# One column block of x by a transposing DMA in the opening of a gated state-space and feed-forward kernel

## The chip, the cores and the metric

The kernel runs on one core of a Trainium2 chip. The metric is the device time of one execution in microseconds; the figure shown is the median of three timed runs. A profiled execution of the same kernel was recorded as well, and its trace is what is read below. Engines are named as the profile names them: PE is TensorE (PEld its weight loads), DVE is VectorE, ACT is ScalarE, POOL is GpSimd, SP is SyncE, which only issues DMAs here. A "q" behind an engine's name means its instruction queue, as in ACTq.

## The reference

```python
x = A_x                                    # 1 x 2048 x 448, bf16
g = sigmoid((x * gate_w).sum(-1, keepdims=True))
# a: a diagonal complex state space of 448 states
dt = exp(log_dt); Lam_bar = exp(dt * Lam)
B_bar = ((Lam_bar - 1.0) / Lam)[:, None] * Bmat
h[t] = Lam_bar * h[t-1] + x[t] @ B_bar.T           # for all 2048 steps
a = 2.0 * real(h @ Cmat.T) + x * Dskip
# b: a feed-forward block, 448 -> 1792 -> 448
b = silu(x @ w1) @ w2
out = g * a + (1 - g) * b
```

Every product with x on TensorE needs x with its 448 features on the partitions, so x is transposed once. The feed-forward block's first product (x times `w1`, then Silu) is the first large piece of work.

## The kernel before

**Layout.** Two neighbouring time steps stand in one row: x is seen as 1024 rows of 896 numbers (`x2`), the even step in columns 0 to 447, the odd one in 448 to 895. `XT` holds x transposed: for each of even and odd three blocks of 128 features and a remainder block, for 1024 rows each. A feature dimension of 448 is three blocks of 128 and 64 left over. The remainder block holds columns 384 to 511 of x2 for the even steps, so that its lower 64 partitions are even features 384 to 447. `XR` is a copy of the 64 remainder features on the other 64 partitions: products with the remainder run as two 64-row matmuls beside each other, one from `XT` (lower half) and one from `XR` (upper half).

**The order of the work** is written out by hand. A tracker records every operation with the buffers it reads and writes (`T.op`, `T.dma`) and puts a wait in front of it where needed; each engine then runs its own list in the order of recording. Plain loads are recorded by `ld` (line 226), transposing DMAs by `ldt` (line 229, always on SP's queue). Two queues issue DMAs, SP's and ACT's.

**The opening**, on which the change bears, handles the first 512 rows of the even steps ("half 0"):

- Lines 275 to 294 issue the first loads, alternately on SP and ACT. `XH` is the first half of the buffer `XN`, seen as four blocks k of 128 rows. XA0 to XA3 are pieces of these four blocks. XB0 (line 282, ACT) holds columns 256 to 511 of blocks 0 and 1, XB1 (line 286, SP) columns 384 to 511 of blocks 2 and 3. Between them go the loads of `w1` (`W1E`): columns 0 to 767 first (`W1Ej0` in two pieces, `W1Ej1`, `W1Ej2`), then on SP and ACT in turn the remainder rows (`W1Er0` on SP, `W1Er1` on ACT), columns 768 to 1279 (`W1Ed0` on SP, `W1Ed2` on ACT), the remainder rows of the later columns (`W1Es0`, `W1Es1`), and columns 1280 to 1791 (`W1Ee0`, `W1Ee1`).
- Line 292 is a one-column Exp that makes ACT load its table of Exp early. Lines 300 and 301 issue, on ACT, the loads of `gate_w` and `Dskip`, each broadcast to 128 partitions (`GWB`, `DB`).
- Line 308 makes SP wait for both remainder loads (`gE`). Then come SP's transposing DMAs: half 1 of the even steps (`XTe1`, `XTer1`), four for the B matrices (`BT`), the plain load of the rest of half 0 (`load_xn(0)`, columns 512 to 895), four for the odd steps, and the plain load of half 1.
- Half 0 of the even steps is transposed on TensorE instead: `turn_k` (line 491) transposes one 128x128 block of `XH` into PSUM, and VectorE copies it to `XT` (lines 501 and 507). The blocks' keys are XTe00, XTe01, XTe02 and, for the remainder block, XTe03.
- `ffn1_first` (line 433) multiplies feature blocks 0, 1 and 2 with the first six column blocks of `w1` as they arrive, between the transposes. Line 472 is a small product that puts the state space's vectors on the partitions; from it VectorE and ACT make the coefficients (`dt`, `phf`, `ar`, `mag`, then `phr`, `fr` and on to the phases, which GpSimd also works on).
- Lines 535 and 536 transpose the remainder block, `turned_x(3)` (line 570) copies it to `XT`, and line 571 copies its lower half from PSUM to the upper half of `XR`. Line 572 is a one-column Silu that loads ACT's Silu table.
- `ffn1_rem` (line 447) adds the remainder's products, three pairs, and `ffn1_act` (line 455) applies Silu to two PSUM banks at a time.

From then on `pair` and `lanes` (line 365) run all further products of `w1` and of B as pairs of 64-row matmuls; the first such pair reads `W1Ed0`, `W1Ed2`, and for its remainder `W1Es0` and `W1Es1`. Later the gate reads `XH` (`gate`, line 650), and `skip` (line 658) multiplies it with `DB`; `xblock` says which loads these wait for.

Of the kernel before, what the change touches and what calls it, by code (L numbers as in the profile page):

```python
# [8 lines left out]
AF = mybir.ActivationFunctionType  # L9
# [141 lines left out]
def gated_mix(nc, A_x, A_Lambda_re, A_Lambda_im, A_B_re, A_B_im, A_C_re, A_C_im, A_log_dt,  # L151
              A_Dskip, B_x, B_w1, B_w2, gate_w, out):
    with ExitStack() as ctx:
        E = ctx.enter_context
        T = Tracker(nc, ctx)

        def sb(name, shape, dtype):
            return E(nc.sbuf_tensor(name, list(shape), dtype))

        x2 = A_x[0].rearrange("(k i) d -> k (i d)", i=2)  # L160
        out2 = out[0].rearrange("(k i) d -> k (i d)", i=2)

        XT = sb("XT", [128, 8, NK], BF16)
# [7 lines left out]
        XR = sb("XR", [128, NK], BF16)  # L171
# [4 lines left out]
        XN = sb("XN", [128, 2 * NKT * D], BF16)  # L176
        AT = [sb(f"AT{i}", [128, NFB, 512], BF16) for i in range(2)]
        OT = sb("OT", [128, 4, D], BF16)
        GWB = sb("GWB", [128, D], BF16)
        DB = sb("DB", [128, D], BF16)  # L180
        JK = sb("JK", [128, 2], BF16)
# [7 lines left out]
        ID = sb("ID", [128, 128], BF16)  # L189
# [5 lines left out]
        HP = sb("HP", [128, 1], F32)  # L195
# [25 lines left out]
        ps = E(nc.psum_tensor("ps", [128, 8, 512], F32))  # L221
# [3 lines left out]
        def ld(eng, dst, src, key, group=None):  # L225
            return T.dma(eng, lambda e: e.dma_start(dst, src), writes=[key], group=group)  # L226

        def ldt(dst, src, key, reads=(), group=None, also=()):
            return T.dma("sp", lambda e: e.dma_start_transpose(dst, src), reads=reads,
                         writes=[key, *also], group=group)  # L230
# [4 lines left out]
        def swap_xr(eng, h, odd):  # L235
            hs = slice(h * 512, (h + 1) * 512)
            if odd:
                T.op(eng, lambda e: e.tensor_copy(XR[0:64, hs], XT[64:128, 7, hs]), reads=XO[h][1],
                     writes=[f"XR{h}b"])
            else:  # L240
                T.op(eng, lambda e: e.tensor_copy(XR[64:128, hs], XT[0:64, 3, hs]), reads=XE[h][1],
                     writes=[f"XR{h}a"])
# [7 lines left out]
        def row(v):  # L250
            return v.rearrange("(o n) -> o n", o=1)

        XH = XN[:, 0:8 * D].rearrange("p (k c) -> p k c", k=4)
        XA = ["XA0", "XA1", "XA2", "XA3", "XB0", "XB1"]
        FA, FB = 768, 1280
        x0 = x2[0:512, 0:512].rearrange("(k p) c -> p k c", p=128)

        def ld_w(eng, j, f0=0, f1=FA, key=""):
            ld(eng, W1E[:, j, f0:f1], B_w1[j * 128:(j + 1) * 128, f0:f1], f"W1Ej{j}{key}")
# [4 lines left out]
        def ld_w3(eng, j0, j1, f0, f1, key):  # L264
            ld(eng, W1E[:, j0:j1, f0:f1], B_w1[j0 * 128:j1 * 128, f0:f1].rearrange("(j p) f -> p j f", p=128),
               f"W1E{key}{j0}")

        def ld_wr(eng, c, later):
            p = slice(64 * c, 64 * c + 64)
            if later:  # L270
                return ld(eng, W1E[p, 3, 384:896].rearrange("p (n f) -> p n f", n=2),
                          B_w1[384:448, FA:].rearrange("p (n c f) -> p n c f", n=2, c=2)[:, :, c, :], f"W1Es{c}")
            return ld(eng, W1E[p, 3, 0:384], B_w1[384:448, 384 * c:384 * c + 384], f"W1Er{c}")

        for k, eng in enumerate(("sp", "act")):
            ld(eng, XH[:, k, 0:256], x0[:, k, 0:256], XA[k])
        for c, eng in enumerate(("sp", "act")):
            ld_w(eng, 0, 384 * c, 384 * c + 384, c)
        for k, eng in ((2, "sp"), (3, "act")):
            ld(eng, XH[:, k, 0:384], x0[:, k, 0:384], XA[k])  # L280
        ld_w("sp", 1)
        ld("act", XH[:, 0:2, 256:512], x0[:, 0:2, 256:512], XA[4])
        for i, (eng, v) in enumerate((("sp", A_log_dt), ("sp", A_Lambda_re), ("act", A_Lambda_im))):
            ld_row(eng, i, v)
        ld_w("act", 2)
        ld("sp", XH[:, 2:4, 384:512], x0[:, 2:4, 384:512], XA[5])
        gE = [ld_wr(eng, c, False) for c, eng in enumerate(("sp", "act"))]
        ld_w3("sp", 0, 2, FA, FB, "d")
        ld_w3("act", 2, 3, FA, FB, "d")
        for c, eng in enumerate(("sp", "act")):  # L290
            ld_wr(eng, c, True)
        T.op("act", lambda e: e.activation(JK[:, 0:1], HP[:, :], AF.Exp), reads=["HP"], writes=["JK0"])
        ld_w3("sp", 0, 1, FB, F_FF, "e")
        ld_w3("act", 1, 3, FB, F_FF, "e")
        BTK = [f"BT{i}" for i in range(4)] + ["BTz"]
# [1 line left out]
        def ld_b(dst, src, key):  # L297
            ld("act", dst[:, :], row(src).partition_broadcast(128).rearrange("p o n -> p (o n)"), key)

        ld_b(GWB, gate_w, "GW")  # L300
        ld_b(DB, A_Dskip, "DB")

        def load_xn(h):
            c0 = 0 if h else 512
            ld("sp", XN[:, 8 * h * D:8 * (h + 1) * D].rearrange("p (k c) -> p k c", k=4)[:, :, c0:],
               x2[h * 512:(h + 1) * 512, c0:].rearrange("(k p) c -> p k c", p=128), f"XN{h}")

# [5 lines left out]
        for i, src in enumerate((A_B_re, A_B_im)):  # L313
# [15 lines left out]
             writes=["IOTA"])  # L329
# [128 lines left out]
        def ffn1(c, f0=0, ahead=None):  # L458
            for fb in range(f0, NFB, 2):
                pair(*ffn1_pair(c, fb), last=(c == 3 and fb == NFB - 2))  # L460
                if ahead and fb == 8:
                    ahead()
                yield
# [23 lines left out]
        xp = [ps[:, b, 0:256].bitcast(BF16) for b in PB]  # L487

        def turn_k(j, k, b=None):
            b = PB[j] if b is None else b  # L490
            T.op("pe", lambda pe: pe.transpose(  # L491
                ps[:, b, 0:256].bitcast(BF16)[:, k * 128:(k + 1) * 128], XH[:, k, j * 128:(j + 1) * 128], ID[:, :]),
                reads=[XA[k if j < 2 or (j == 2 and k > 1) else 4 + k // 2], "ID"], writes=[f"ps{b}"])

        def turn_x(j, i):
            for k in (2 * i, 2 * i + 1):
                turn_k(j, k)
# [6 lines left out]
        def turned_x(j, i=None, b=None):  # L504
            c, key = (slice(0, 512), f"XTe0{j}") if i is None else (slice(256 * i, 256 * i + 256), f"XTe0{j}{i}")
            b = PB[j] if b is None else b
            T.op("dve", lambda e: e.tensor_copy(XT[:, j, c], ps[:, b, 0:256].bitcast(BF16)[:, c]),
                 reads=[f"ps{b}"], writes=[key])
# [13 lines left out]
        for k in (2, 3):  # L522
# [7 lines left out]
            reads=["pv", "ps7"], writes=["PV"])  # L530
# [1 line left out]
            turn_x(2, i)  # L532
        turned_x(2)
        next(first)
        for i in range(2):
            turn_x(3, i)

        names = {}

        def pc(n):  # L540
            if n not in names:
                names[n] = len(names)
            return names[n]

        def col(n):
            i = pc(n)
            return P[:, i, :]
# [7 lines left out]
        def pts(o, a, s1, s2, op0, op1, ra):  # L555
            T.op("dve", lambda e: e.tensor_scalar(col(o), a, s1, s2, op0, op1), reads=ra, writes=[o])

        def ptt(o, a, b, op, ra):
            T.op("dve", lambda e: e.tensor_tensor(col(o), a, b, op), reads=ra, writes=[o])

        def pact(o, a, f, ra, scale=1.0, bias=0.0):
            T.op("act", lambda e: e.activation(col(o), a, f, bias=bias, scale=scale),
                 reads=ra, writes=[o])
# [3 lines left out]
            col("phf"), LIM, 1.0 / TWO_PI, col("dt"), ALU.mult, ALU.mult), reads=["PV", "dt"], writes=["phf"])  # L567
        ptt("ar", col("dt"), LRE, ALU.mult, ["dt", "PV"])
        pact("mag", col("ar"), AF.Exp, ["ar"])
        turned_x(3)  # L570
        T.op("dve", lambda e: e.tensor_copy(XR[64:128, 0:512], xp[3][0:64, :]), reads=["ps7"], writes=["XR0a"])
        T.op("act", lambda e: e.activation(JK[:, 0:1], HP[:, :], AF.Silu), reads=["HP"], writes=["JK0"])
        pts("phr", col("phf"), MAGIC, -MAGIC, ALU.add, ALU.add, ["phf"])
        ptt("fr", col("phf"), col("phr"), ALU.subtract, ["phf", "phr"])
        pts("nfr", col("fr"), -1.0, None, ALU.mult, ALU.bypass, ["fr"])
# [6 lines left out]
            reads=["f2"] + SGN, writes=["f2s"])  # L582
# [55 lines left out]
        def xblock(b):  # L638
            v = XN[:, 4 * b * D:4 * (b + 1) * D].rearrange("p (k c) -> p k c", k=4) if b > 1 else \
                XH[:, :, b * D:(b + 1) * D]  # L640
            return v, [*(XA if b < 2 else []), *([f"XN{b // 2}"] if b else [])]

        def block(tile):
            return tile // 4 if tile > 7 else tile % 2
# [1 line left out]
        def gate():  # L646
            for b in range(4):
                v, ks = xblock(b)
                o, ws = xg(b)
                T.op("dve", lambda e, v=v, o=o: e.tensor_tensor(  # L650
                    o, v, GWB[:, :].unsqueeze(1).to_broadcast([128, 4, D]), ALU.mult),
                    reads=ks + ["GW"], writes=ws)
                yield

        def skip():
            for b in range(4):
                v, ks = xblock(b)
                T.op("dve", lambda e, v=v: e.tensor_tensor(
                    v, v, DB[:, :].unsqueeze(1).to_broadcast([128, 4, D]), ALU.mult),
                    reads=ks + ["DB"], writes=[f"XD{b}"] + ks)  # L660
                yield
# [12 lines left out]
             writes=["BTz"] + BTK[2:4])  # L674
# [486 lines left out]
        f = ffn1(2)  # L1161
# [100 lines left out]
```

## Time and profile before

| what | value |
|---|---|
| timed runs | 136.61, 136.64, 136.76 us; median 136.64 |
| profiled execution | 136.72 us, of which the span from first to last instruction is 135.3 |
| TensorE | busy 131.9 us, 97% of the span |
| VectorE | busy 114.2 us, 84% |
| ScalarE | busy 93.7 us, 69% |
| GpSimd | busy 15.1 us, 11% |
| DMA | 24928 packets, 11.95 MB; 16851 packets under 512 B |

Times in the trace count from the first instruction of the span. The span is shorter than the execution's time by what lies before and after it. The 40 slices of the page are 3.4 us each, and a digit is the busy share in tenths:

```profile
PE   7899999999999999999999999999999999999993
DMA  4999979999897220000122000000000000222123
```

TensorE is busy in every slice from the second on; the DMA engines are busy in the first dozen slices and hardly afterwards. Matmuls are pipelined, so that a busy TensorE is not TensorE at its peak. The granted TensorE clock was 1.0 over the whole span.

### The profile page before, as it was taken

The numbers are of one execution on the slowest core, as the hardware profiler recorded it, in microseconds if no ns is written. First come the engines' busy times: TensorE is split into PE (matmuls) and PEld (weight loads), VectorE is DVE, ScalarE is ACT, GpSimd is POOL, SyncE is SP. The second block draws the span as 40 slices with busy tenths as digits, with TensorE's granted clock in tenths as the row PEclk, the third lists the DMA queues.
The fourth block names the chain that finished last, engine by engine and source line by source line (L and its number), as shares of the span: only waits on it lengthen the run. The fifth ranks groups of instructions, "written<-read, shape, count | busy, mean of one in ns | idle before, by whom it ended". The sixth has DMA issues, their size and how long they took to land.

```text
span 135.3 us, 2630 instructions
## 1 busy us (share of the span) xinstructions
PE 131.9 (97%) x1072; PEld 65.7 (49%) x1073; DVE 114.2 (84%) x152; ACT 93.7 (69%) x146; POOL 15.1 (11%) x32
## 2 busy tenths in 40 slices
PE   7899999999999999999999999999999999999993
PEld 7554444444444554444445544445555555555552
DVE  1467898917899798999999999999999999994554
ACT  0369888899939999768999597797113437879200
POOL 7108768050000000000000000000000000000000
DMA  4999979999897220000122000000000000222123
GB/s 109 273 278 162 157 153 244 181 286 300 251 184 123 55 62 0 0 0 0 44 56 60 5 0 0 0 5 0 0 0 0 0 0 7 100 89 81 68 78 126
DMA packets 24928, 11.95 MB, mean 88 GB/s; under 512 B 16851, under 2 KB 24406, under 8 KB 24918
## 3 DMA queue, kind: packets, MB, share of 16 engines
q1 hardware_dynamic: 22996, 10.43, 32.3%
q10 hardware_dynamic: 1922, 1.37, 3.6%
q8 instruction: 8, 0.13, 0.4%
q14 instruction: 2, 0.02, 0.0%
HBM read 5.51 MB, written 1.84 MB: 54 GB/s over the span
## 4 chain that ended last, share of the span: by engine, by line
PE 94%; DMA 3%; DVE 1%; ACTq 1%; issue 0%
PE ps L365 44%; PE ps L794 16%; PE ps L809 16%; PE ps L1047 15%; DMA XN<-in_A_x_dram 3%; PE ps L433 3%; DVE TMPS L1071 1%; ACTq L226 1%; PE ps L491 1%; PE ps L447 1%; PE ps L472 0%
## 5 line engine op out<-in xcount | busy, mean ns | idle before, releaser
L365 PE MATMUL ps<-XT,W1E 64*128 64x512 bf16 x325 | 41.3, 376 | 0.0
L455 ACT ACTIVATE AT<-ps 128x1024 bf16<-128x1024 f32 x28 | 28.2, 1019 | 7.4 <-PE ps L365 7.2
L365 PEld LDWEIGHTS ps<-XT,W1E 64*128 64x128 bf16 x325 | 16.9, 94 | 19.0 <-ACT AT L455 0.3
L365 PE MATMUL ps<-XT,BT 64*128 64x512 bf16 x156 | 22.4, 376 | 0.0
L809 PE MATMUL ps<-W,AT 64*128 64x448 bf16 x224 | 21.5, 349 | 0.0
L794 PE MATMUL ps<-W,AT 128*128 128x448 bf16 x112 | 21.4, 353 | 0.0
L794 PEld LDWEIGHTS ps<-W,AT 128*128 128x128 bf16 x112 | 10.9, 98 | 10.5 <-issue 0.4
L809 PEld LDWEIGHTS ps<-W,AT 64*128 64x128 bf16 x224 | 10.9, 94 | 10.4
L838 ACT ACTIVATE BT<-ps,GT 128x448 bf16<-128x448 f32 x8 | 5.1, 634 | 13.2 <-PE ps L794 13.2
L894 DVE SCALAR_TENSOR_TENSOR HS<-VE,P,ps 128x512 bf16<-128x512 bf16 (+1 forms) x13 | 9.6, 780 | 3.9 <-PE ps L365 3.9
L365 PEld LDWEIGHTS ps<-XT,BT 64*128 64x128 bf16 x156 | 8.1, 94 | 9.3 <-DVE HS L894 0.4
L938 DVE TENSOR_TENSOR_SCAN G<-P,Q 128x1024 f32<-128x1024 f32 (+1 forms) x6 | 11.4, 1923 | 0.0
L1047 PE MATMUL ps<-CO,VE 128*128 128x448 bf16 (+2 forms) x63 | 11.1, 332 | 0.0
L1047 PE MATMUL ps<-CO,HS 128*128 128x448 bf16 x56 | 11.1, 352 | 0.0
L365 PE MATMUL ps<-XR,W1E 64*128 64x512 bf16 x25 | 9.2, 376 | 0.0
L1047 PEld LDWEIGHTS ps<-CO,VE 128*128 128x128 bf16 x63 | 6.0, 98 | 4.8
L1047 PEld LDWEIGHTS ps<-CO,HS 128*128 128x128 bf16 x56 | 5.5, 98 | 5.1
L891 DVE TENSOR_TENSOR Q<-G,COS 128x2048 bf16<-128x2048 f32 (+1 forms) x4 | 7.0, 1755 | 0.1
L891 DVE TENSOR_TENSOR Q<-G,SIN 128x2048 bf16<-128x2048 f32 (+1 forms) x4 | 7.0, 1750 | 0.0
L856 ACT ACTIVATE VE<-ps 128x1024 bf16<-128x1024 f32 x6 | 6.1, 1020 | 1.2 <-PE ps L365 1.2
L858 ACT ACTIVATE ps<-VE,P 128x1024 f32<-128x1024 bf16 x6 | 6.7, 1118 | 0.2
L894 DVE SCALAR_TENSOR_TENSOR VE<-HS,P,FP 128x512 bf16<-128x512 bf16 (+1 forms) x7 | 6.6, 976 | 0.1
(123 smaller groups left out, 179.1 us busy)
## 6 DMA issues: line engine op xcount, KB each, us to landing
W<-in_B_w_dram SPq DMA_DIRECT2D x2, 784.0 KB, 6.6
XN<-in_A_x_dram SPq DMA_DIRECT2D x1, 896.0 KB, 5.1
out_dram<-OT SPq DMA_DIRECT2D x8, 112.0 KB, 1.7
out_dram<-TMPS SPq DMA_DIRECT2D x7, 112.0 KB, 1.7
HS<-HS SPq DMA_DIRECT2D x4, 128.0 KB, 2.3
XN<-in_A_x_dram SPq DMA_DIRECT2D x1, 384.0 KB, 3.7
W1E<-in_B_w_dram SPq DMA_DIRECT2D x1, 256.0 KB, 5.5
W1E<-in_B_w_dram ACTq DMA_DIRECT2D x1, 256.0 KB, 5.0
```

The lines of the kernel that those rows point to most:

```text
L365: ins = pe.matmul(ps[:, bank, :], w(p, j), xh(odd, h, j, p), start=start and j == js[0], stop=stop and j == js[-1], skip_group_check=seeded)
L433: T.op("pe", lambda pe, fb=fb, bank=bank, j=j, h=h, c=c: pe.matmul(ps[:, bank, c], W1E[:, j, ff(fb) * 128:(ff(fb) + 1) * 128], XT[:, j, c] ...
L455: T.op("act", lambda e: e.activation(a[:, fb:fb + n, :], ps[:, bank:bank + n, :], AF.Silu), reads=[f"ps{bank + i}" for i in range(n)], wri ...
L794: ins = pe.matmul(ps[:, bank, 0:D], a[:, fb, q * 128:(q + 1) * 128], W2[:, ff(fb), :], start=(first and fb == 0), stop=(fb == NFB - 1), sk ...
L809: ins = pe.matmul(ps[:, bank, 0:D], a[p, fb, q * 128:(q + 1) * 128], W2[p, ff(fb), :], start=(start and fb == 0), stop=(not start and fb = ...
L838: T.op("act", lambda e: e.activation(bs(tile), ps[:, bank, 0:D], AF.Copy, scale=sc), reads=[f"ps{bank}", "GT2" if h else "GRI"], writes=ks)
L856: T.op("act", lambda e: e.activation(VE[:, m:m + 2, hs], ps[:, b[0]:b[0] + 2, :], AF.Copy), reads=[f"ps{i}" for i in b], writes=vs)
L858: T.op("act", lambda e: e.activation(ps[:, o[0]:o[0] + 2, :], VE[:, m:m + 2, hs], AF.Copy, scale=c1("lr", pt)), reads=vs + ["lr"], writes= ...
L891: T.op("dve", lambda e: e.tensor_tensor(o, a, b, op), reads=reads, writes=writes)
L894: T.op("dve", lambda e: e.scalar_tensor_tensor(o, a, s, b, ALU.mult, ALU.add), reads=reads, writes=writes)
L938: T.op("dve", lambda e: e.tensor_tensor_scan(G[:, c, w], rb, Q1[:, c, w], init, ALU.mult, ALU.add), reads=[f"Q1{c}", "rr", f"G{c}"], write ...
L1047: ins = pe.matmul(ps[:, bank, c], state(kt, odd, m), CO[:, m, c], start=False, stop=(m == YB[-1]), skip_group_check=True)
```

## The change

The remainder block of half 0 of the even steps now comes by a transposing DMA on SP, in the place where the load XB1 stood. XB0 shrinks to columns 256 to 383; XB1 goes; the four TensorE transposes of this block and the two copies out of PSUM go, and `XR`'s upper half is copied from `XT` by `swap_xr`, a copy between two SBUF buffers on VectorE. Columns 384 to 511 of half 0 in their plain form, which the gate and the skip product need, come with `load_xn(0)`, which now begins at column 384; so block 0 of these now waits for that load too. The one-column Exp moves up in ACT's list, before the loads of `W1E`'s remainder rows. The two broadcast loads move down in ACT's list, behind the one-column Silu.

```diff
-        XA = ["XA0", "XA1", "XA2", "XA3", "XB0", "XB1"]
+        XA = ["XA0", "XA1", "XA2", "XA3", "XB0"]
...
-        ld("act", XH[:, 0:2, 256:512], x0[:, 0:2, 256:512], XA[4])
+        ld("act", XH[:, 0:2, 256:384], x0[:, 0:2, 256:384], XA[4])
...
         ld_w("act", 2)
-        ld("sp", XH[:, 2:4, 384:512], x0[:, 2:4, 384:512], XA[5])
+        ldt(XT[:, 3:4, 0:512], x2[0:512, 384:512], "XTe03")
+        T.op("act", lambda e: e.activation(JK[:, 0:1], HP[:, :], AF.Exp), reads=["HP"], writes=["JK0"])
         gE = [ld_wr(eng, c, False) for c, eng in enumerate(("sp", "act"))]
...
-        T.op("act", lambda e: e.activation(JK[:, 0:1], HP[:, :], AF.Exp), reads=["HP"], writes=["JK0"])
         ld_w3("sp", 0, 1, FB, F_FF, "e")
...
-        ld_b(GWB, gate_w, "GW")
-        ld_b(DB, A_Dskip, "DB")
-
         def load_xn(h):
-            c0 = 0 if h else 512
+            c0 = 0 if h else 384
...
-                reads=[XA[k if j < 2 or (j == 2 and k > 1) else 4 + k // 2], "ID"], writes=[f"ps{b}"])
+                reads=[XA[k if j < 2 or k > 1 else 4], "ID"], writes=[f"ps{b}"])
...
         next(first)
-        for i in range(2):
-            turn_x(3, i)
...
         pact("mag", col("ar"), AF.Exp, ["ar"])
-        turned_x(3)
-        T.op("dve", lambda e: e.tensor_copy(XR[64:128, 0:512], xp[3][0:64, :]), reads=["ps7"], writes=["XR0a"])
+        swap_xr("dve", 0, 0)
         T.op("act", lambda e: e.activation(JK[:, 0:1], HP[:, :], AF.Silu), reads=["HP"], writes=["JK0"])
+        ld_b(GWB, gate_w, "GW")
+        ld_b(DB, A_Dskip, "DB")
...
-            return v, [*(XA if b < 2 else []), *([f"XN{b // 2}"] if b else [])]
+            return v, [*(XA if b < 2 else []), f"XN{b // 2}"]
```

## The prediction

> **What bounds the kernel now.** I read the page's busy shares first: TensorE is busy for 97% of the span, VectorE for 84%. Then the chain of work that ended last, in order of time (start us, length us, what):
>
> ```profile
> 1.71 3.59 DMA XN<-in_A_x_dram
> 5.30 0.05 issue
> 5.34 0.23 PE ps L491
> ...
> 7.75 0.59 PE ps L433 x2
> 8.34 0.22 PE ps L491 x4
> 8.56 1.29 PE ps L433 x6
> 9.86 0.76 PE ps L447 x6
> 10.61 31.76 PE ps L365 x294
> ```
>
> The last load that TensorE waits for is the fourth row block of x (issued at 1.71 on ScalarE's queue, landed at 5.30). From 5.34 to 132.76 the chain is TensorE alone. So nothing after 10.6 us can be shortened by this change: a gain must start the line-365 stream earlier, and a loss must start it later or open a hole in it. The four transposes that go are the 0.22 us at 8.34.
>
> Next the timeline around them (start, length, engine, line, what, idle before it):
>
> ```profile
> 3.27 0.41 SPq L226 DMA_DIRECT2D XN<-in_A_x_dram  x1
> 3.73 2.79 SPq L226 DMA_DIRECT2D W1E<-in_B_w_dram  x4
> 8.60 3.94 SPq L229 DMA_TRANSPOSE XT<-in_A_x_dram  x2
> 8.14 0.16 DVE L559 TENSOR_TENSOR P<-P,PV 128x4 f32<-128x4 f32 x1
> 9.06 0.42 DVE L571 COPY XR<-ps 64x512 bf16<-64x512 bf16 x1
> 5.61 1.28 ACT L292 ACT_TABLE_LOAD   x1 [5.61 <-DVE XT L501]
> 5.68 0.55 ACTq L226 DMA_DIRECT2D W1E<-in_B_w_dram  x1
> 9.85 0.20 ACT L572 ACTIVATE JK<-HP 128x1 bf16<-128x1 f32 x1
> 10.22 1.02 ACT L455 ACTIVATE AT<-ps 128x1024 bf16<-128x1024 f32 x1 [0.17 <-PE ps L447]
> ```
>
> The load that goes is SP's at 3.27; the transposing DMA takes its place, ahead of four W1E loads. Third, the list of DMA issues in narrow windows, for single loads (KB, us from issue to landing). SP's W1E load of columns 768 to 1279 (key W1Ed0, issued 4.34, 256 KB) took 5.5 us and landed at 9.82; TensorE needs it for the first pair of the line-365 stream. The remainder rows on SP (W1Er0, issued 3.73, 48 KB) took 4.9 us, to 8.6; W1Es0 (5.21) 5.0, to 10.2. The XB1 load took 4.0, to 7.3. Single transposes of the same size as the new one:
>
> ```profile
> XT<-in_A_x_dram SPq DMA_TRANSPOSE x1, 6.1
> XT<-in_A_x_dram SPq DMA_TRANSPOSE x1, 2.9
> ```
>
> The first was issued at 10.15 behind a busy queue, the second at 21.70 in a quiet stretch. Last, busy time by stretches (from:to, length, busy time of PE, PEld, DVE, ACT, POOL, then clock, DMA share, GB/s):
>
> ```profile
> 8.00:9.00 1.00, 1.00 (x9) 0.58 (x8) 0.70 (x4) 0.65 (x2) 0.00 (x0) 1.00 1.02 320
> 9.00:10.00 1.00, 1.00 (x6) 0.31 (x6) 0.87 (x6) 0.99 (x2) 0.00 (x0) 1.00 0.97 238
> 11.50:12.40 0.90, 0.90 (x12) 0.39 (x10) 0.89 (x1) 0.90 (x4) 0.89 (x1) 1.00 1.12 84
> 12.50:13.50 1.00, 1.00 (x14) 0.41 (x10) 0.43 (x1) 1.00 (x2) 1.00 (x1) 1.00 1.28 282
> 14.90:15.80 0.90, 0.90 (x12) 0.39 (x8) 0.90 (x3) 0.45 (x1) 0.90 (x1) 1.00 1.11 30
> ```
>
> The DMA engines have no spare time in the first 10 us (shares near 1). Transposes alone can move 282 GB/s (12.5 to 13.5). But in two stretches with transposes under way, the first with the broadcasts' packets still between them, the engines stayed occupied (shares 1.12 and 1.11) and moved only 84 and 30 GB/s for 0.9 us. I call these holes.
>
> **The parts, one by one.** All against the profiled execution: 136.72 us, of which 135.3 is the span; the median of the three timed runs is 136.64.
>
> TensorE loses four transposes, 0.22 us. The next matmuls (line 433, the third column block) also read the copy XTe02, which VectorE makes from 7.73 to 8.15; with 0.05 us of hand-over, as at 5.30 to 5.34, they can start at 8.20, against 8.40 now: 0.20 gained. Behind them ScalarE's first big Silu activation starts at 10.22, and its end (11.24) releases the banks of the second line-365 pair. It can't start before the Silu table's dummy ends at 10.05, and nothing in that chain moves (dt, ar, mag hang on the matmuls before the removed transposes). So 0.16 of the 0.20 passes. I take **-0.17 us**.
>
> VectorE loses two PSUM copies of 0.42 (XTe03, and XR's upper half at 9.06) and gets one copy SBUF to SBUF, 0.29 by the same copy at 16.38. Its coefficient chain could start about 0.9 us earlier; TensorE waits for nothing from it before 12 us, so this is worth 0. In return VectorE now waits, in order, for the transpose's landing, with the whole phase chain queued behind, for which GpSimd waits at 10.65.
>
> When does the transpose land? Bounds from the rows: 3.27+2.9 = 6.2 and 3.27+6.1 = 9.4. It sits in a full queue, so it is nearer the second; XB1 took 4.0 in that place with half the bytes. I take 8.5. Copy 0.29 and two hand-overs of 0.05: 8.9, before the 9.59 at which line 447 would want it. Even 9.4 gives 9.8, about where line 447 starts today (9.79).
>
> The Trainium skill (DMA: Bandwidth & Descriptors, Latency and other measured facts) gives a DMA transpose an effective 261 GB/s; 128 KB would be 0.50 us by that page, an estimate, the queue behind it would hardly feel it, and the sum would stay at the -0.17.
>
> The loads behind it on SP: W1Er0, W1Ed0, W1Es0, W1Ee0. Issue: a one-block transpose holds SP for 1.26 us (21.70 to 22.96) or 2.39 (10.15 to 12.54), against 0.41, so each of the four is issued 0.85 to 1.98 later. W1Ed0's 5.5 us to landing, against 2.1 for the kernel's first load, says that over 3 us of it is queueing; the later issue is covered, and I count it at 0 (without that cover it costs the 0.85). Bytes: 128 KB stands ahead of them in place of 64. The rate over 5 to 9 us is 323, 251, 299, 320, mean 298 GB/s; with ScalarE's queue taking half, 64 KB cost 0.44 us. The holes: either none (the stretch at 282), or one like 11.5 to 12.4, which loses 0.9x(1-84/282) = 0.63 us, or one more like 14.9 to 15.8, 0.9x(1-30/282) = 0.80. A transpose that starts among full plain queues is nearest to the first hole, where plain packets were still under way; I take 0.63. Back come the broadcasts, which after the change are issued behind the Silu table (from 8.6 instead of 6.3): the rate fell to 238 in the 0.8 us before W1Ed0 landed, so 0.8x(1-238/320) = 0.20 is theirs at most. W1Ed0: 9.82+0.44+0.63-0.20 = **10.69**. The first line-365 matmul started at 10.45; now it starts at 10.69+0.05 = 10.74: **+0.29 us** instead of -0.17. The wait decides from a landing at 10.20 on. W1Es0, 0.87 later, is at 11.07, wanted 0.65 after the stream's start: 11.39. W1Er0, at 8.6+0.87 = 9.5, is wanted at 9.59: just hidden.
>
> ScalarE's queue: XB0 is half as long (64 KB less ahead of its W1E loads: earlier). The Exp table load moves ahead of four W1E issues. The row at 5.68 shows an issue in the middle of a table load, so it costs the queue only a dispatch: issue starts at 5.68 after one that began at 4.93 and took 0.66, a gap of 0.09.
>
> The Trainium skill (ScalarE: Activation LUTs, What ACT_TABLE_LOAD costs) adds a drain of 1380 ns to each load, 2.66 us in all; held back by that much, W1Ed2 would come to 11.7 instead of 9.1 and the kernel would lose 1.3 us; in the trace the dummy activation runs at 6.91, straight after the 1.28, so no drain shows.
>
> The broadcasts' issues (0.49 and 0.45) follow the dispatch at 8.56 and are over by 9.6, before the Silu activation at 10.05. They are wanted at 23.5 and 24.7: 0.
>
> Later: SP waits for both remainder loads before its first transposes at 8.60, so all that follows moves by W1Er0's 0.9. XTer1, landed at 16.2, is copied at 16.38 and used from XR at 18.44; the B copies end at 20.9 and are used at 22.97; x's second half: copies at 25.81 and 27.52, used from 29.2 on. All have 1.3 us or more to spare. The first XN load grows by 128 KB (0.46 us at 282 GB/s) and the gate's first product, at 23.51, now waits for it: 22.7+0.46+0.9 = 24.1, 0.6 late for VectorE, whose next wanted result is the 25.81 copy with 3.4 us to spare. All 0, unless SP slips by over 1.3 us.
>
> Sum: +0.29. On the median, 136.64+0.29 = **136.93 us**.
>
> **Rivals.** *Hidden* (0.38): no hole, or the straggling DMA engine isn't the one that the transpose burdens. W1Ed0 lands at 9.82+0.44-0.20 = 10.06, inside the 10.20: 136.64-0.17 = 136.47, no change that can be measured (0.2%, or 0.27 us, is about what a measurement here can tell). For it: the four loads' landings are queueing, and 128 KB went and 128 KB came. Against it: the two holes.
>
> *The transpose itself* (0.08): it lands after 9.65 and line 447 waits through the copy; at 10.0 line 447 starts at 10.39, +0.60: 137.24. It needs 6.7 us, more than any row of x's transposes.
>
> *Faster* (0.12), the other side: the start at 5.34 is set by one load, and TensorE idles 0.44 before it. Should the lighter traffic (the load behind it halved) land this block 0.3 earlier, the whole opening moves with it, up to W1Ed0: with 9.82 it is 9.87 instead of 10.45. Price -0.47: 136.17; it decides from 0.10 earlier. Against it: both loads that changed stand behind that block in their queues.
>
> **Numbers.** Late W1E loads 0.42, own range 136.9 to 137.6 (the second hole adds 0.80, to 137.7). Slower: 0.42+0.08 = 0.50; within 0.2%: 0.38; faster: 0.12. The range, 136.4 to 137.6, takes in the hidden case and leaves out the faster one and the case of two holes with a late issue, 0.18 together.
>
> **What would show it.** Right: L365's first matmul starts near 10.7, preceded by idle time that a W1E load ends; the W1E load on SP lands after 10.2; a stretch of 0.5 us or more between 5 and 9 with a full DMA share and under 150 GB/s. Hidden: L365 starts near 10.28, no TensorE idle after 5.4. The third: idle before L447, ended by the XR copy. Faster: the first idle at 5.34 shorter. I would be wrong altogether if a hole opened in the stream after 12 us, or if W1Ej2 or XB0 on ScalarE's queue came late (landed 6.9 and 6.1, wanted at 8.3 and 7.3).

## The result, and the profile after

The changed kernel takes 137.31 us, the median of 20 runs (136.53 to 137.93), against 136.62 (136.29 to 137.06, 20 runs) for the kernel before on the same chip. The ratio is 1.0044, 95% interval [1.0029, 1.0058]: slower by about 0.6 us. The profiled execution took 137.58 us, with a span of 136.2; it is the third longest of the 20, so what its trace shows is somewhat more than the median's loss. Line 365 is line 362 after the change, 447 is 444, 433 is 430, 491 is 488, 472 is 469.

First the chain of work that ended last (start us, length us, what):

```profile
3.28 1.22 SPq L229
...
4.55 0.67 SPq L226
...
5.27 5.99 DMA W1E<-in_B_w_dram
11.30 31.93 PE ps L362 x294
```

Before, the last load on the chain was the fourth row block of x at 5.30, and TensorE ran alone from there. Now the chain goes over the transposing DMA's issue on SP (the 1.22 us at 3.28), the issue of W1Er0 behind it, and the load of W1Ed0 (issued 5.27, landed 11.26). The line-362 stream starts at 11.30; before it started at 10.45. That is 0.85 us of the 0.9 by which the span grew. From the stream's start to the end of the span it is 124.9 us here and 124.85 before: nothing else moved the time of this execution.

The timeline around the place (start, length, engine, line, what, idle before it and what ended it):

```profile
3.69 1.28 ACT L287 ACT_TABLE_LOAD   x1 [3.69 <-DVE XT L498]
4.99 0.20 ACT L287 ACTIVATE JK<-HP 128x1 bf16<-128x1 f32 x1
8.05 0.29 DVE L241 COPY XR<-XT 64x512 bf16<-64x512 bf16 x1
9.90 0.39 PE L444 MATMUL ps<-XT,W1E 64*128 64x512 bf16 x1 [0.42 <-DMA W1E<-in_B_w_dram]
11.30 1.03 PE L362 MATMUL ps<-XT,W1E 64*128 64x512 bf16 x7 [0.58 <-DMA W1E<-in_B_w_dram]
```

The transpose itself is in time: VectorE copies its lower half to XR at 8.05, and TensorE could have started line 444 at about 9.4. TensorE waits twice, each time for a load of W1 that stands behind the transpose on SP: at line 444 for W1Er0, and before the stream for W1Ed0. The list of DMA issues gives the three (KB, us from issue to landing; the transpose was issued at 3.28, W1Er0 at 4.55, W1Ed0 at 5.27):

```profile
XT<-in_A_x_dram SPq DMA_TRANSPOSE x1, 4.7
W1E<-in_B_w_dram SPq DMA_DIRECT2D x1, 48.0 KB, 5.3
W1E<-in_B_w_dram SPq DMA_DIRECT2D x1, 256.0 KB, 6.0
```

So they landed at 7.99, 9.86 and 11.26. The last two came at 8.6 and 9.82 before.

Last, the stretches of half a microsecond in which the transpose is under way (from:to, length, busy time of PE, PEld, DVE, ACT, POOL, then clock, DMA share, GB/s):

```profile
5.50:6.00 0.50, 0.50 (x6) 0.45 (x7) 0.25 (x2) 0.00 (x0) 0.00 (x0) 1.00 1.44 224
6.00:6.50 0.50, 0.50 (x7) 0.32 (x5) 0.17 (x2) 0.00 (x0) 0.00 (x0) 1.00 0.89 161
6.50:7.00 0.50, 0.50 (x6) 0.26 (x5) 0.00 (x0) 0.00 (x0) 0.00 (x0) 1.00 1.13 202
7.00:7.50 0.50, 0.45 (x10) 0.38 (x10) 0.22 (x2) 0.09 (x1) 0.00 (x0) 1.00 1.21 179
```

The same four stretches of the kernel before:

```profile
5.50:6.00 0.50, 0.50 (x6) 0.32 (x5) 0.28 (x2) 0.39 (x1) 0.00 (x0) 1.00 0.96 285
6.00:6.50 0.50, 0.50 (x6) 0.45 (x6) 0.40 (x2) 0.50 (x1) 0.00 (x0) 1.00 0.93 239
6.50:7.00 0.50, 0.50 (x6) 0.25 (x4) 0.00 (x0) 0.49 (x2) 0.00 (x0) 1.00 0.93 262
7.00:7.50 0.50, 0.50 (x10) 0.38 (x9) 0.01 (x1) 0.12 (x1) 0.00 (x0) 1.00 0.92 311
```

That was 274 GB/s on average; after the change it is 192. The DMA engines are at least as occupied as before (shares of 1.17 and 0.94 over the 2 us) and move less. (The profile books the bytes and the time of a packet in the stretch in which the packet starts, so a share above 1, or a low one behind it, is to be read together with its neighbours.) What is missing, some 83 GB/s for 2 us, takes 0.6 us to move at 274 GB/s. From here on I call such a stretch, occupied engines with little moved, a hole, as the prediction did.

### The profile page after: what moved, and what is told of

The parts are those of the page before. It is cut to its first block, busy times and chain, and to the rows that moved or that the text cites. A ratio compares the mean times of both kernels' runs of the same rounds, so it can differ in the third digit from the quotient of the medians.

```text
span 136.2 us, 2621 instructions
## 1 busy us (share of the span) xinstructions
PE 131.9 (97%) x1068; PEld 65.4 (48%) x1069; DVE 113.6 (83%) x151; ACT 93.9 (69%) x146; POOL 15.3 (11%) x32
## 4 chain that ended last, share of the span: by engine, by line
PE 90%; DMA 4%; SPq 3%; DVE 1%; issue 0%
PE ps L362 43%; PE ps L790 16%; PE ps L805 16%; PE ps L1043 15%; DMA W1E<-in_B_w_dram 4%; SPq L226 2%; SPq L229 1%; DVE TMPS L1067 1%
```

## The experiments

The theory after the result: the transposing DMA makes a hole, wherever it is put and whatever its size, and TensorE pays where loads that it wants soon stand behind the transpose in its queue. The rivals: it is the bytes or the place in SP's queue (more KB ahead of W1Ed0); it is the broadcasts, which moved too; or it is only the longer issue on SP. Each run is compared with runs of the kernel before on the same chip. In each, the stream of line 362 (365 in the kernel before; the line shifts by a few in others) is where to look: the span less the stream's start is 124.8 to 125.0 in all but two of them, which have a wait inside the stream, so that a late start is the whole loss.

**The same block as a plain load of 128 KB.** The kernel before, with XB0 cut and the whole block in XB1's place, transposed on TensorE as before.

```diff
-        ld("act", XH[:, 0:2, 256:512], x0[:, 0:2, 256:512], XA[4])
+        ld("act", XH[:, 0:2, 256:384], x0[:, 0:2, 256:384], XA[4])
...
-        ld("sp", XH[:, 2:4, 384:512], x0[:, 2:4, 384:512], XA[5])
+        ld("sp", XH[:, 0:4, 384:512], x0[:, 0:4, 384:512], XA[5])
...
-                reads=[XA[k if j < 2 or (j == 2 and k > 1) else 4 + k // 2], "ID"], writes=[f"ps{b}"])
+                reads=[XA[5 if j == 3 else k if j < 2 or k > 1 else 4], "ID"], writes=[f"ps{b}"])
```

> The kernel before, with the same block of x (columns 384 to 511 of all 512 rows, 128 KB) loaded plainly in one load at XB1's place on SP, and XB0 on ACT cut to columns 256 to 383: the bytes and places of the change without a transposing DMA; TensorE keeps its four transposes, broadcasts and Exp stay. Theory (the transposing DMA itself opens a hole of about 0.8 us in all traffic, on top of 0.44 us for 64 KB more ahead on SP's queue): no stretch of 0.5 us under 150 GB/s between 5 and 7 us, W1Ed0 lands at 9.8 to 10.3, TensorE waits at most 0.1 us, time within 0.2% of before. Rival (bytes and place on SP's queue alone): W1Er0 near 9.9 and W1Ed0 near 11.2 as in the changed kernel, time +0.5 to +0.8 us.

Measured: 136.54 us against 136.50, ratio 1.0002 [0.9986, 1.0018]. W1Er0 landed at 8.09 and W1Ed0 at 9.67, both earlier than in the profile of before, and TensorE never waited for them. There is no hole: the four stretches from 5.5 to 7.5 moved 240 GB/s on average with a share of 0.92, and the least of them is

```profile
6.50:7.00 0.50, 0.50 (x5) 0.25 (x4) 0.00 (x0) 0.49 (x2) 0.00 (x0) 1.00 0.83 212
```

Nor is it the size of the packets: the records have 512 packets of 256 bytes for this load and 512 for the transpose, and the median one takes 18 ns in both. So 128 KB in this place, with 64 KB less on ScalarE's queue, cost nothing: it is neither the bytes nor the place, but that the DMA transposes (or that it takes longer to issue).

**The broadcasts' move alone**, in the kernel before.

```diff
-        ld_b(GWB, gate_w, "GW")
-        ld_b(DB, A_Dskip, "DB")
...
         T.op("act", lambda e: e.activation(JK[:, 0:1], HP[:, :], AF.Silu), reads=["HP"], writes=["JK0"])
+        ld_b(GWB, gate_w, "GW")
+        ld_b(DB, A_Dskip, "DB")
```

> The kernel before, with only the two broadcast loads moved behind the Silu table. Theory (transposing DMA): W1Ed0 lands at 9.5 to 9.8, a little earlier since the broadcasts start later; TensorE's line-365 stream still starts at 10.45; time within 0.1% of before. Rival (the broadcasts' new place, where their packets meet the last W1E loads, makes W1Ed0 late): W1Ed0 after 10.4, time +0.3 us or more.

Measured: 136.83 against 136.50, ratio 1.0020 [1.0001, 1.0040]. The profiled execution is one of the shorter ones (136.55 us); the stream started at 10.30 in it and TensorE did not wait. In it the first two transposes of half 1 land 1.2 us later than before (15.31 and 17.40 against 14.15 and 16.23), which TensorE does not feel there. If the median's 0.3 us is real, this profile does not show where it goes; it stays open.

**The change without the broadcasts' move.**

```diff
+        ld_b(GWB, gate_w, "GW")
+        ld_b(DB, A_Dskip, "DB")
...
-        ld_b(GWB, gate_w, "GW")
-        ld_b(DB, A_Dskip, "DB")
```

> The changed kernel, with the two broadcast loads back at their old place on ACT's queue, before the dt activation. Theory: W1Er0 and W1Ed0 as late as in the changed kernel (9.9 and 11.3) or up to 0.3 us later, time +0.6 to +0.9 us against before. Rival (the broadcasts' new place is the cause): W1Ed0 before 10.3, time at or below before.

Measured: 137.06, ratio 1.0047 [1.0025, 1.0069]: the loss is there as with the broadcasts moved (1.0044). Its stretches show a deeper hole than the changed kernel's:

```profile
6.00:6.50 0.50, 0.50 (x5) 0.20 (x3) 0.00 (x0) 0.00 (x0) 0.00 (x0) 1.00 1.05 96
6.50:7.00 0.50, 0.33 (x2) 0.00 (x0) 0.07 (x1) 0.00 (x0) 0.00 (x0) 1.00 0.89 111
```

And a line of its timeline:

```profile
7.24 0.24 PE L472 MATMUL ps<-ID,R 128*128 128x4 bf16 x4 [0.41 <-DVE R L466]
```

Here the hole held up the three small rows of the state space's vectors, which landed at 6.90, and TensorE waited 0.41 us for the product of line 472 that reads them; then W1Er0 (9.21) and W1Ed0 (10.30) were in time, and W1Es0 (11.31) cost 0.16. The hole is the same kind; which load is caught in it differs between these two profiles. The loss does not need the broadcasts' move.

**The transpose behind W1Er0 and W1Ed0.**

```diff
-        ldt(XT[:, 3:4, 0:512], x2[0:512, 384:512], "XTe03")
...
         ld_w3("sp", 0, 2, FA, FB, "d")
+        ldt(XT[:, 3:4, 0:512], x2[0:512, 384:512], "XTe03")
         ld_w3("act", 2, 3, FA, FB, "d")
```

> The changed kernel, with the transposing DMA issued on SP behind W1Er0 and W1Ed0 instead of ahead of them. Theory (what is queued behind the transpose is late): W1Er0 lands near 8 and W1Ed0 near 9.5, both in time; the transpose, issued near 4.7, lands at 8.8 to 9.6 and TensorE waits for XR's copy up to 0.3 us at line 444, W1Es0 lands near 11; time from -0.1 to +0.3 us against before, clearly below the changed kernel. Rival (the hole comes wherever the transpose stands and holds all loads): W1Ed0 still after 10.5, time +0.5 us or more.

Measured: 137.59, ratio 1.0075 [1.0050, 1.0100]. A line of the timeline, and one stretch:

```profile
11.19 0.37 PE L444 MATMUL ps<-XT,W1E 64*128 64x512 bf16 x1 [1.85 <-DVE XR L241]
```

```profile
8.50:9.00 0.50, 0.50 (x4) 0.20 (x2) 0.00 (x0) 0.50 (x1) 0.00 (x0) 1.00 0.23 44
```

W1Er0 (7.35) and W1Ed0 (9.49) were in time, as the theory has it, and the hole moved with the transpose, to 8.0 to 9.5 (44 GB/s at its deepest). But I had expected the transpose at 8.8 to 9.6, and it landed at 10.73, 6.2 us after its issue at 4.53: TensorE waited 1.85 us for its copy. So the time I expected was missed. At the 149 GB/s that the prediction gave one queue, the 304 KB ahead of the transpose take 2.1 us, an estimate, and it landed 2.0 to 2.7 us later than in the change's place (7.99 to 8.71): the bytes ahead account for most of that, and I had allowed 0.8 to 1.6.

**A quarter of the transpose.** The kernel before, with one transposing DMA of 32 KB more, ahead of XB1. Its output is written over by a later one.

```diff
+        ldt(XT[:, 3:4, 512:640], x2[512:640, 384:512], "XTer1")
         ld("sp", XH[:, 2:4, 384:512], x0[:, 2:4, 384:512], XA[5])
```

> The kernel before with its four TensorE transposes and all its loads, and one more, small transposing DMA (128 rows by 128 columns, 32 KB, a quarter of the change's) on SP ahead of XB1; what it writes is written again later by the larger transpose of the same rows. Theory (a transposing DMA holds the DMA engines that reach it until the last engine has, so that the hole depends on how far the engines are apart and not on its bytes): all traffic falls below 200 GB/s for about 0.5 us between 5 and 7 us, W1Ed0 lands at 10.2 to 10.9, time +0.1 to +0.5 us. Rival (the cost goes with the transposed bytes): 0.1 us at most, no fall, time within 0.1% of before.

Measured: 138.28, ratio 1.0127 [1.0103, 1.0152]. The timeline has two waits of TensorE at the stream's start (line 366 here), and before them one of 0.17 for XB1, which landed at 8.42:

```profile
11.20 0.82 PE L366 MATMUL ps<-XT,W1E 64*128 64x512 bf16 x6 [0.40 <-DMA W1E<-in_B_w_dram]
12.59 0.39 PE L366 MATMUL ps<-XT,W1E 64*128 64x512 bf16 x1 [0.57 <-DMA W1E<-in_B_w_dram]
```

The kernel lost more with 32 KB transposed than with 128 KB. The transpose landed 4.2 us after its issue (the larger one 4.7), W1Ed0 at 11.15 and W1Es0 at 12.54. That is also above what my theory gave it; here XB1 stands behind the transpose as well, all of SP's loads are issued 1.2 us later or more, and the TensorE work was not made less. But the run does not show that the hole is as dear at a quarter of the size. From 5.5 to 7.5 its stretches moved 221 GB/s on average, 179 at the least, and W1Er0, issued 1.49 us later than before, landed at 8.59, as before (8.58). The two loads that TensorE waits for most landed at the end of a second slow time, 10.0 to 12.5, in which the core moved 80 to 174 GB/s: there they meet the broadcasts (packets of 896 bytes on ScalarE's queue, up to 0.76 us each) and, from 10.96, the transposes of half 1. So the run settles neither how the price goes with the bytes nor how the loss divides between the hole and the late issue; it shows that a later issue of 1.49 us can be covered.

**The transpose first in SP's queue.**

```diff
+        ldt(XT[:, 3:4, 0:512], x2[0:512, 384:512], "XTe03")
         for k, eng in enumerate(("sp", "act")):
...
-        ldt(XT[:, 3:4, 0:512], x2[0:512, 384:512], "XTe03")
```

> The changed kernel with the transposing DMA as the very first DMA on SP's queue. Theory (engines apart): nothing is under way in front of it on SP, so all engines reach it nearly together: no packet of over 0.4 us around it, it lands 2.8 to 3.5 us after its issue; the loads behind it come 0.9 to 1.8 us late, TensorE begins its transposes that much later, and the time is +0.5 to +1.5 us; no further hole, W1Er0 and W1Ed0 not later than 9.5 and 10.8. Rival (a transpose always opens a hole, for instance by being set up in the DMA engines): the hole stands near 3 us and all loads are a further 0.6 to 0.9 us late, time +1.5 to +2.5 us.

Measured: 139.26 (2 runs), ratio 1.0198 [1.0161, 1.0235], worse than either theory said. The transpose landed 3.65 us after its issue, the shortest here, with a short hole (122 GB/s from 3.0 to 3.5). TensorE's first work then waited 1.94 us for the first row blocks of x and 0.62 for the first of W1. After that it waited for no load: no idle at line 444 or before the stream, which started at 12.87. W1Er0 landed at 8.83 and W1Ed0 at 11.12, 0.25 and 1.30 us later than before, but TensorE, itself 2.4 us late, wanted them later still. So the loads next to the transpose pay here, and whether the others recover can't be told.

**The transpose on ScalarE's queue**, behind W1Ej2 there (so W1Er1, W1Ed2 and the rest of ScalarE's loads stand behind it, and none of SP's).

```diff
-        ldt(XT[:, 3:4, 0:512], x2[0:512, 384:512], "XTe03")
+        gX = T.dma("act", lambda e: e.dma_start_transpose(XT[:, 3:4, 0:512], x2[0:512, 384:512]), writes=["XTe03"])
...
-        T.wait_all("sp", gE)
+        T.wait_all("sp", gE + [gX])
```

> The changed kernel with the transposing DMA on ScalarE's queue in the same place of the list (behind W1Ej2), SP's own transposes waiting for its landing too. Theory (the hole holds the DMA engines, both queues): a fall below 200 GB/s for 0.5 us or more as in the changed kernel, with SP's loads held as well; W1Er1 and W1Ed2, now behind it, land at 8.5 to 10 and W1Ed0, not behind it, at 9.8 to 10.6; time +0.1 to +0.7 us. Rival (only what is queued behind the transpose is late): W1Ed0 at 9.4 to 9.8, W1Ed2 at 9.5 to 10.1, in time; time -0.2 to 0 us against before.

Measured: 137.53, ratio 1.0061 [1.0042, 1.0081]. One stretch:

```profile
6.50:7.00 0.50, 0.50 (x6) 0.26 (x5) 0.00 (x0) 0.00 (x0) 0.00 (x0) 1.00 0.90 104
```

The two that follow moved 128 and 131 GB/s. The late loads changed sides: SP's W1Er0 (7.78) and W1Ed0 (9.76) were in time, ScalarE's W1Er1 landed at 10.55 (before: 7.1) and W1Ed2 at 11.14 (before: 9.1). TensorE waited 1.15 us before line 444; the profile names a VectorE operation as the releaser, but of what line 444 reads, W1Er1 and the copy of the transpose (landed 10.04) came last. The hole is there with the transpose in the other queue, and in it packets of both queues stand. The longer issue alone does not explain this: W1Er1 was issued 1.37 us later than before (5.07 and 3.70) and landed 3.47 us later, and the 64 KB more ahead of it on its queue take 0.44 us at the prediction's rate, an estimate.

**Less behind the transpose.** The changed kernel with the split of the two last pieces of W1 swapped: SP loads one feature block of columns 768 to 1279 (128 KB) and ScalarE's queue two.

```diff
-        ld_w3("sp", 0, 2, FA, FB, "d")
-        ld_w3("act", 2, 3, FA, FB, "d")
+        ld_w3("sp", 0, 1, FA, FB, "d")
+        ld_w3("act", 1, 3, FA, FB, "d")
...
-        ld_w3("sp", 0, 1, FB, F_FF, "e")
-        ld_w3("act", 1, 3, FB, F_FF, "e")
+        ld_w3("sp", 0, 2, FB, F_FF, "e")
+        ld_w3("act", 2, 3, FB, F_FF, "e")
...
```

The names of these pieces (W1Ed1 and W1Ee2 for W1Ed2 and W1Ee1) change with it in the list of what the products wait for.

> The changed kernel with the next W1E loads shared out otherwise: of columns 768 to 1279 SP loads one block of rows instead of two and ScalarE two instead of one, and the other way round for columns 1280 to 1791; 128 KB less stand on SP's queue behind the transpose before TensorE's stream can start. Theory: W1Er0 still near 9.2 to 9.9, the loads of columns 768 to 1279 at 10.0 to 10.6 on both queues; time +0.1 to +0.4 us against before, below the changed kernel's +0.6. Rival (TensorE's late start is W1Er0's alone): time as in the changed kernel.

Measured: 136.80 against 136.46, ratio 1.0025 [1.0009, 1.0041]. Two stretches, and the only wait in the timeline that is left at this place:

```profile
6.00:6.50 0.50, 0.50 (x5) 0.23 (x4) 0.00 (x0) 0.00 (x0) 0.00 (x0) 1.00 0.70 108
...
7.00:7.50 0.50, 0.45 (x6) 0.21 (x4) 0.43 (x2) 0.21 (x1) 0.00 (x0) 1.00 1.14 117
```

```profile
9.49 0.39 PE L444 MATMUL ps<-XT,W1E 64*128 64x512 bf16 x1 [0.25 <-DMA W1E<-in_B_w_dram]
```

The hole is as deep as ever, but W1Ed0 (10.06) and the piece on ScalarE's queue (9.93) are there when the stream wants them; it starts at 10.15 without a wait. Only W1Er0 (9.45) still costs something. The profiled execution, 136.53 us, is at the low end of its 12 runs.

**The same split in the kernel before**, as a control for that run (same edit).

> The kernel before with the same swapped split as the run with the swapped split of W1Ed and W1Ee (SP loads W1Ed for one feature block, 128 KB, ScalarE's queue for two). A control: it says how much of that run's 136.80 is the split and how much the change. Theory (the change costs because SP's W1 loads stand behind the transpose): the kernel before has no TensorE idle that the split could take away (its loads land before they are wanted), so the time stays within 0.2 us of the kernel before, ratio 0.998 to 1.0015; W1Ed0 lands before 9.6 and W1Ed1 before 10.2. Then the change, with the split, costs still 0.1 to 0.4 us. Rival (the split by itself makes this kernel faster or slower, whatever the transpose does): 0.3 us or more off either way, and the gain of the swapped split over the changed kernel has nothing to do with the transpose.

Measured: 136.73 against 136.38, ratio 1.0017 [1.0000, 1.0034]. W1Ed0 landed at 9.21, the other piece at 9.18, as expected, and TensorE did not wait for them; the ratio is a little above what I expected. With the swapped split the kernel without the transpose takes 136.73 and the one with it 136.80: the ratios differ by 0.0008, 0.1 us, at the foot of the 0.1 to 0.4 that I expected. The two intervals together leave some 0.3 us either way, an estimate. So with less behind it the transpose costs 0.1 ± 0.3 us where it cost 0.6 ± 0.2: the loss is smaller as far as can be told, and not shown to be gone. The split itself made the kernel without the transpose slower, if anything.

**Only W1Er0 ahead of the transpose**, with the swapped split: the version that I thought could beat both kernels.

```diff
-        ldt(XT[:, 3:4, 0:512], x2[0:512, 384:512], "XTe03")
-        T.op("act", lambda e: e.activation(JK[:, 0:1], HP[:, :], AF.Exp), reads=["HP"], writes=["JK0"])
-        gE = [ld_wr(eng, c, False) for c, eng in enumerate(("sp", "act"))]
+        gE = [ld_wr("sp", 0, False)]
+        ldt(XT[:, 3:4, 0:512], x2[0:512, 384:512], "XTe03")
+        T.op("act", lambda e: e.activation(JK[:, 0:1], HP[:, :], AF.Exp), reads=["HP"], writes=["JK0"])
+        gE.append(ld_wr("act", 1, False))
```

> The changed kernel with the swapped split, and with the transpose one place later on SP: behind W1Er0, ahead of W1Ed0 (now 128 KB). Theory (TensorE waited for W1Er0 and W1Ed0 because they stood behind the transpose, whose standing period moves with it): W1Er0 lands at 7.2 to 8.2 instead of 9.4 to 9.9; the transpose, issued at 3.7, lands at 8.3 to 9.3, and as line 444 wants its copy XR at about 9.2, TensorE waits 0 to 0.5 us there; W1Ed0 lands before 10.3 and the stream does not wait. Time 136.4 to 136.9, ratio 0.999 to 1.002: the best form of the change, at most as fast as the kernel before. Rival (the change's own gain of 0.16 us shows once no load is late): 136.2 to 136.4, ratio 0.997 to 0.9985. A third possibility, the transpose is drawn out as it was behind W1Ed0 (landing after 10): TensorE waits 0.9 us or more before line 444, time above 137.2.

Measured: 137.79 against 136.38, ratio 1.0094 [1.0075, 1.0113]: the third possibility. The timeline's wait for the transpose's copy:

```profile
10.87 0.37 PE L445 MATMUL ps<-XT,W1E 64*128 64x512 bf16 x1 [1.64 <-DVE XR L241]
```

48 KB ahead of it and an issue 0.6 us later (3.88) made the transpose land at 10.41, against 8.64 in the run before last: 1.8 us later. W1Er0 was in time (8.07). The places tried give, from issue to landing of the 128 KB: 3.65 us first in the queue; 4.7, 5.4 and 5.4 in the change's place; 6.5 behind W1Er0; 6.2 behind W1Ed0; 6.3 on the other queue. In this kernel no place that was tried has both the transpose and its followers in time.

Taken together: from 5.5 to 7.5 us the four kernels with no transpose among the first loads moved 274, 240, 264 and 269 GB/s (the kernel before, the plain 128 KB, the broadcasts' move, the swapped split), with shares of 0.92 to 0.95. The three with the 128 KB transpose in the change's place moved 192, 143 and 157 GB/s, with shares of 1.17 to 1.27. Engines that are short of work because of a late issue should show lower shares; these are higher, which speaks for the hole.

## Why the prediction was right, and which term was too small

The direction and the mechanism held: late W1 loads behind the transpose on SP, the stream's start moved, nothing after it. The time, 136.93, is 0.4 us short of the median and inside the range. That the sum came this near is in part luck: two of its terms do not show (see W1Ed0 below), the opening gained 0.29 us that was not counted on, and with the broadcasts back the same loss came by other loads than W1Ed0. Point by point:

- **TensorE's gain.** Predicted: line 447 could start 0.20 earlier. From the product of line 472 to the remainder's matmuls the kernel before takes 2.58 us (7.21 to 9.79). After, TensorE is through at 9.48 by the profile's idle time, which means a start at 9.41 (a start lies 0.07 before the modelled end of the matmul ahead, as in the run with the 128 KB load): 6.92 to 9.41, or 2.49. With the swapped split it is 6.69 to 9.17 by the same reckoning, with the broadcasts back 7.24 to 9.72, 2.48 both. So 0.10 was gained. The copy XTe02 starts at 7.45 and ends at 7.87, and the six matmuls behind it load their weights from 7.99, not 0.05 later as I took. Another 0.29 of gain came from the opening: line 472's product stood 0.29 earlier, the fourth row block of x having landed at 4.81 instead of 5.30. That is what the rival *Faster* waited for. I can't put it down to the change: this load landed at 4.36 in the run that moves the broadcasts alone, where everything in the queues ahead of it and behind it is as before, and at 4.61 in the run with the plain 128 KB, whose stream still started at 10.45.
- **The transpose's landing**: 8.5 predicted; 7.99, 8.71 and 8.64 in the three runs with it in this place. Right; line 444 did not wait for it in the changed kernel, and the rival *The transpose itself* was out, until the transpose was moved behind other loads.
- **The later issue**: 0.85 to 1.98 predicted; W1Ed0 was issued 0.93 later (4.34 to 5.27). Whether it is covered by the queueing, as I took it, can't be separated from the hole here; in the run with 32 KB a later issue of 1.49 cost W1Er0's landing nothing.
- **W1Er0, "just hidden" at 9.5: this step failed.** It landed at 9.86 while TensorE was ready at 9.41 instead of 9.59, so the stream's start moved by 0.49 there. I had given it the same 0.87 as W1Ed0 (bytes, one hole, less the broadcasts), which left 0.1 us to spare; its delay was 1.27. In the two other runs with the transpose in this place it was 0.63 and 0.86 (9.21 and 9.45).
- **W1Ed0: the term that was too small.** 10.69 predicted, 11.26 measured: a delay of 1.44 in place of 0.87. Its pieces fare worse than the sum. The 0.44 for bytes does not show: a plain load of the same 128 KB delayed nothing. The 0.20 that the broadcasts should give back can't be told: W1Ed0 landed 0.36 earlier in the run that moves them alone, but with the transpose the ratio is the same at the old place and the new. So nearly all of the 1.44 goes with the transposing, where I had 0.63 for one hole. The missing transfer in the stretches above is worth 0.6, about that hole; the later issue (0.93) is of the size of the rest, but no run shows it alone. The run with the broadcasts back put W1Ed0 at 10.30, earlier than predicted, so the delay varies, from 0.5 to 1.4. The records show what varies: a load's landing comes in 16 parts and counts with the last. The eighth part of W1Ed0 came at 8.23 before, at 9.08 after the change and at 9.93 with the broadcasts back, the last at 9.82, 11.26 and 10.30. The load as a whole is late in both, by 0.85 and 1.70 us; but its parts lie 2.2 us apart after the change (2.4 before) and 0.5 us with the broadcasts back.
- **The sum** goes on from the stream's start: -0.38 (0.10 and 0.29, rounded) at line 444, +0.49 for W1Er0, and +0.74 for W1Ed0 (line 444's first matmul at 9.90 would let the stream start 0.66 later, at 10.56; it started at 11.30) make +0.85.
- **The sign I named**, a stretch of 0.5 us under 150 GB/s with a full share, is not in the changed kernel's profile by its letter (161 is the least); it is in those of the runs with the broadcasts back (96 and 111 at shares of 1.05 and 0.89), with the swapped split (117 at 1.14) and on the other queue (104 to 131 at 0.88 to 1.05).
- **ScalarE and what comes later**: as predicted. The dummy activation follows the table load directly (3.69 + 1.28 = 4.97, started at 4.99), the issues go on during it, and TensorE has no idle after the stream's start that the change made.

What is argued and not shown: why the engines stand. In the records of single packets, many packets of both queues last until one common moment near the end of such a stretch (6.43 in the changed kernel) and then all go on; what they wait for is not in the records. In the run with the transpose behind W1Ed0 the traffic was low, too, from 5.5 to 6.5 (138 and 134 GB/s, at shares of 0.77 and 0.54), before the first packet of the transpose at 7.39; why is open. Nor was the transpose's longer issue (1.2 us against 0.4) tried without a transpose, so how much of a load's delay is the issue's stays open.

## What to carry to other kernels

A transposing DMA among busy plain loads is paid for by its neighbours: before it replaces a load, look which transfers stand next behind it in its queue and when TensorE wants each, and give every one of them the delay (0.5 to 1.4 us for the first two loads here) with room to spare; the 0.1 us that the prediction left W1Er0 was none. Four TensorE transposes that are in the way for 0.1 us are cheaper than that where an opening is bound by its loads. If it must be there, lightening what follows it in that queue seems to help (ratio 1.0025 in place of 1.0044, with intervals that overlap). Setting it behind a load made its own landing late: by 1.8 us with 48 KB ahead of it, by 2.0 to 2.7 with 304 KB.

## What the runs showed of the hardware that I had not expected

- The landing hardly goes with the size. A transposing DMA of 32 KB took 4.2 us to land in the place where one of 128 KB took 4.7 to 5.4. The Trainium skill (DMA: Bandwidth & Descriptors, Latency and other measured facts) gives transposes an effective 261 GB/s with a non-contiguous middle dimension, 0.50 us for the 128 KB by an estimate from it. With the transpose first in the queue its packets took 0.56 us on the mean of 16 engines, close to that; but it landed 3.65 us after the issue there and up to 6.5 elsewhere, and W1Ed0 behind it lost 0.5 to 1.4 us.
- A plain load of 128 KB in place of 64, with 64 KB less on the other queue, delayed nothing behind it (W1Ed0 at 9.67 against 9.82), although the DMA share is near 1 there.
- The hole reaches both queues: with the transpose on ScalarE's queue the core as a whole moved 104 to 131 GB/s for 1.5 us, against 262 to 311 in the same stretches of the kernel before. The long packets are the transpose's own and those of the other queue's loads: ScalarE's in the changed kernel, SP's here.
- One load's landing can hang on one packet. Of the 16 parts of W1Er0's landing, 15 were in by 8.59 in the changed kernel; one of its packets, of 768 bytes, took 1.77 us (7.44 to 9.21; the median one took 0.04), three more followed it, and the load landed at 9.86.
